# Earlier convolution steps, one product in fixed order, and room between statistics and norm rows in a gated long-convolution and SwiGLU layer

## The chip, the cores and the metric

The kernel runs on one core of a Trainium2 chip. Its time is device time in microseconds (us), the median of several runs. The engines named below are PE (TensorE, matrix products; PEld is its weight load), DVE (VectorE, elementwise), ACT (ScalarE, activations and casts), POOL (GpSimd) and SP (the engine whose queue issues the transfers). SBUF is the working memory of 128 partitions, PSUM the memory that PE writes its products to.

## The reference

A block of a transformer with 2048 tokens of 576 features, in two halves. The first is a long convolution along the tokens, the second a gated feed-forward layer with 4608 hidden features. Six rows (sa, ca, ga, sb, cb, gb) come from a condition vector.

```python
k_shift = sum_t k_pad[:, t:t+S, :] * shift_k[:, ks-1-t]        # 4 taps
kv = k_shift * v
y  = irfft(rfft(pad(kv)) * rfft(pad(ssm_k)))[:S] + kv * ssm_D  # causal, along the tokens
A(q, ...) = q * y
B(x) = (silu(x @ w1) * (x @ w3)) @ w2

h = layernorm(x) * (1 + ca) + sa
x = x + ga * A(h, k, v, shift_k, ssm_k, ssm_D)
h = layernorm(x) * (1 + cb) + sb
x = x + gb * B(h)
```

The layer norm has no weights of its own: it subtracts the mean and divides by sqrt(variance + 1e-5).

## The kernel before

The tokens are cut into eight blocks of 256 for the convolution and into four row blocks of 512 for the feed-forward layer. The convolution of a block works in a transformed domain: PE transforms the block's kv (spectrum X) and the block's filter (W, combined to V) by matrix products; block s is then the sum over j of X[j] * V[s - j], which DVE forms by one multiply and one add of 128 x 3456 elements for each pair; PE transforms the sum z back. So later blocks have more pairs. X and V of early blocks are written to memory and fetched again.

```python
def pair(self, X, V, s, last=False):
    nc = self.nc
    if s not in self.accs:                       # the first product of a block goes straight to z
        self.accs[s] = self.acc.tile([P, 6, D], BF16, name=f"z{s % 2}", tag=f"z{s % 2}")
        nc.vector.tensor_mul(self.accs[s][:], X[:], V[:])
        yield 2.0
        return
    z = self.accs[s]
    p = self.prod.tile([P, 6, D], BF16, name="p", tag="p")
    with self.behind(nc.vector) if last else nullcontext():
        nc.vector.tensor_mul(p[:], X[:], V[:])
    yield 2.0
    nc.vector.tensor_add(z[:], z[:], p[:])
    yield 2.0

def behind(self, engine):                        # what is traced inside comes after the engine's
    last = [i for i in self.nc.cur_bb.bb.instructions if i.engine == engine.engine][-1]
    return self.tc.issue_after(last)             # last traced instruction
```

The order of instructions on each engine is set when the kernel is built. A scheduler orders them by dependencies and by the order in which they are traced, and may move an instruction up; `behind` forbids that for what is traced inside it.

The convolution of the next two blocks is laid beside the feed-forward layer of the present row block. It is a generator: each `yield` says what its step costs in us; a negative number asks for so many us of other steps before it goes on, and `mix` takes these from a second generator. `advance` is called by the feed-forward code after each chunk of work and traces as many steps as its budget pays for.

```python
def advance(self, cost):
    self.due += cost
    while self.due > 0 and self.steps is not None:
        c = next(self.steps, None)
        if c is None:
            self.steps = None
            break
        self.due -= c
        self.spent += c
# in row_blocks: CONV_US = (72.0, 97.0, 108.0) for the convolution beside row blocks 0, 1, 2
            cost = CONV_US[r]
            time = 110.0 * 0.85 - (N1 * 1.03 if r == 0 else 0)
            rate = cost / time
# in stream(): the end of a chunk (128 hidden features for 512 tokens)
        def hide(k):
            ...
            nc.scalar.activation(h3, gus[k][:, 0, :].rearrange("p (a t) -> p a t", a=m), ACT.Silu)
            u = self.hp.tile([P, RB], BF16, name="u", tag="u")
            nc.scalar.copy(u[:], gus[k][:, 1, :])
            nc.vector.tensor_mul(h3, h3, u[:].rearrange("p (a t) -> p a t", a=m))
            del gus[k]
            self.advance(rate * 2.05)
# in down(): after each group of 16 products with w2; all steps that are left come at the sixth group of the second half
                if h == 1 and f0 // W2C == 5 and r + 1 < NRB:
                    self.end()
                    self.turn_all(2 * r + 3)
                ...
                self.advance(rate * W2C * 4 * 0.126)
```

A row block is `stream` (36 chunks: products with w1 and w3, L934 and L945, then silu, cast and product to h) and then `down` (products of h with w2, L1046, in two halves of 288 output features; L1063 reads a finished half from PSUM). The fourth row block runs in `stream_halves` (L1001), with no convolution beside it. PSUM holds four tiles of two banks. Each chunk takes one such tile, and so does each transform.

The last steps of a block of the convolution, `outcome`: the sums' real parts, back transform on PE, residual, statistics of the second norm on ACT, and the norm rows, which PE turns (L574) and which become the next row block's input.

```python
            yield self.real_parts(s)
            yield -waits[0]
            ...                                          # inverse transform, cast to y
            yield -waits[1]
            self.residual(s, y)
            yield 1.5
            if between is not None:
                between()
            ...                                          # (block 1 takes a quicker way here)
                sums = [...]
                for i in range(2):
                    with self.behind(nc.scalar):
                        self.ln_sums(self.xo[s], i, *sums)
                    yield 0.0
                yield -waits[2] / 2
                stats = self.ln_var(*sums, "l2")         # two DVE steps, then a power on POOL
                yield -waits[2] / 2
                r, b = self.ln_shift(*stats)             # one DVE step, l2n
                with self.behind(nc.scalar):
                    self.normed_act(s, r, b)             # four ACT instructions, h2row
            yield -waits[3]
```

The rows of the first norm are made the same way: `gate_stats`, `gate_var` (DVE, then POOL), and `gate_rows` (DVE's `ln_shift`, then two ACT instructions that write hg).

Of the kernel before, what the change touches and what calls it, by code (L numbers as in the profile page):

```python
# [32 lines left out]
N1 = 24  # L33
SPLIT = 2
EPS = 1e-5
EARLY_GETS = 6
# [8 lines left out]
class _Kernel:  # L45
# [277 lines left out]

    def kv_rows(self, s):

        nc = self.nc
        kh, vt = self.kh, self.vt
        kv = self.kvp.tile([P, 2, D], BF16, name="kv", tag="kv")
        tmp = self.kvp.tile([P, 2, D], BF16, name="kvt", tag="kvt")

        def tap(j):
            a = self.shk[:, j, :]
            return bass.AP(tensor=a.tensor, offset=a.offset, ap=[list(a.ap[0]), [0, 2], [1, D]])
        nc.vector.tensor_mul(kv[:], kh[:, 3:5, :], tap(0))
        yield 0.75
        for j in (1, 2, 3):
            nc.vector.tensor_mul(tmp[:], kh[:, 3 - j:5 - j, :], tap(j))  # L337
            nc.vector.tensor_add(kv[:], kv[:], tmp[:])  # L338
            yield 1.5
        nc.vector.tensor_mul(kv[:], kv[:], vt[:])  # L340
        self.kv = kv
        yield 0.75
# [40 lines left out]

    def v_block(self, s):

        nc = self.nc
        W = self.Wl[s]
        V = self.spec.tile([P, 6, D], BF16, name="V", tag="V")
        if s == 0:
            nc.vector.tensor_copy(V[:, 0:6:3, :], W[:, 0:4:2, :])  # L390
            VS = W[:, 1:4:2, :]
        else:
            Wp = self.Wl[s - 1]
            nc.vector.tensor_add(V[:, 0:6:3, :], W[:, 0:4:2, :], Wp[:, 1:4:2, :])
            nc.vector.tensor_sub(V[:, 1:6:3, :], W[:, 1:4:2, :], Wp[:, 0:4:2, :])
            VS = V[:, 1:6:3, :]
        nc.vector.tensor_add(V[:, 2:6:3, :], V[:, 0:6:3, :], VS)
        yield 2.25
        nc.vector.tensor_sub(V[:, 1:6:3, :], VS, V[:, 0:6:3, :])
        self.V[s] = V  # L400
        yield 0.75

    def pair(self, X, V, s, last=False):

        nc = self.nc
        if s not in self.accs:
            self.accs[s] = self.acc.tile([P, 6, D], BF16, name=f"z{s % 2}", tag=f"z{s % 2}")
            nc.vector.tensor_mul(self.accs[s][:], X[:], V[:])  # L408
            yield 2.0
            return  # L410
        z = self.accs[s]
        p = self.prod.tile([P, 6, D], BF16, name="p", tag="p")
        with self.behind(nc.vector) if last else nullcontext():
            nc.vector.tensor_mul(p[:], X[:], V[:])  # L414
        yield 2.0
        nc.vector.tensor_add(z[:], z[:], p[:])  # L416
        yield 2.0
# [58 lines left out]
    def center(self, dst, src, mean, rstd):  # L476
        self.nc.vector.tensor_scalar(dst, src, mean, rstd, op0=ALU.subtract, op1=ALU.mult)

    def behind(self, engine):

        last = [i for i in self.nc.cur_bb.bb.instructions if i.engine == engine.engine][-1]
        return self.tc.issue_after(last)
# [10 lines left out]
    def gate_var(self, s):  # L493
        self.l1[s] = self.ln_var(*self.l1[s])

    def gate_rows(self, s):

        x1 = self.xo[s]
        r, b = self.ln_shift(*self.l1.pop(s))
        hg = self.lnp.tile([P, 2, D], BF16, name="hg", tag="hg")  # L500
# [63 lines left out]

    def normed_act(self, s, r, b):
        row, x1 = self.h2row, self.xo[s]
        for cc in range(2):
            for lo, hi, at in ((0, D, 0), (512, D, D)):
# [170 lines left out]
    def outcome(self, s, fill, waits, between=None, quick=False):  # L739


        def steps():
# [19 lines left out]
            else:  # L762
# [7 lines left out]
                yield -waits[2] / 2  # L770
                r, b = self.ln_shift(*stats)
                with self.behind(nc.scalar):
                    self.normed_act(s, r, b)
            yield -waits[3]
# [11 lines left out]
    def conv_second(self):  # L786
        yield from self.gate_stats(1)
        yield from self.kv_rows(1)
        block = self.v_block(1)
        with self.behind(self.nc.vector):  # L790
            cost = next(block)
        yield cost

        def beside():
            yield from block
            self.gate_var(1)
            yield from self.pair(self.X[0], self.V[1], 1)
        yield from self.mix(self.x_spectrum(1), beside())
        self.mod_piece(5)
# [9 lines left out]
    def conv(self, s0):  # L809
        s1 = s0 + 1  # L810
# [12 lines left out]
        def old():  # L823
            V, X = self.old_v(s0 - 1, s0), self.old_x(1, s0)
            yield from self.pair(X, V, s0)
            for j in range(2, s0):
# [13 lines left out]
        def beside():  # L840
            yield from self.v_block(s1)
            with self.behind(self.nc.sync):
                self.load_kv(s1)
            yield from self.gate_stats(s1)
            if s0 > 2:
                yield from self.pair(X0, self.V[s0], s0)
            self.X1 = self.old_x(1, s0)
            yield from self.pair(X0, self.V[s1], s1)
            self.gate_var(s1)
            self.gate_rows(s0)  # L850
            yield from self.gate(s0)
# [8 lines left out]
        def others():  # L860
            yield from self.kv_rows(s1)
            yield from self.mix(self.x_spectrum(s1), more())
            yield from self.x_sums(s1)
# [35 lines left out]
    def stream(self, r, jobs, rate, size, finish=False):  # L899
# [49 lines left out]
        def hide(k):  # L949
# [7 lines left out]
            del gus[k]  # L957
            self.advance(rate * 2.05)

# [222 lines left out]
```

## Time and profile before

| what | value |
|---|---|
| time, median of 3 runs | 519.06 us (518.48 to 519.46) |
| profiled execution, span | 516.6 us |
| block 0 and set-up | about 0 to 34 us |
| row block 0, first half of its tokens, beside block 1 | about 34 to 67 us |
| row block 0, the rest of its products, beside blocks 2 and 3 | about 67 to 130 us, `down` to 170 |
| row block 1 beside blocks 4 and 5 | about 170 to 291 us, `down` from 248 |
| row block 2 beside blocks 6 and 7 | about 291 to 407 us, `down` from 369 |
| row block 3 | about 407 to 516 us, `down` from 477 |
| one large product or sum on DVE (128 x 3456) | 1.95 us |
| one DVE instruction of 128 x 1152 | 0.75 us |
| one chunk's silu and cast on ACT | 0.60 and 0.59 us |

How to read it: a line number such as L934 is a line of the kernel. In a timeline a line has the start in us, the length, the engine, the operation and what it writes and reads; in brackets stands how long the engine was idle just before it, and what ended that. A group's shape is partitions x elements. An engine's idle time costs something only where the chain that sets the end runs through it.

### The profile page before, as it was taken

To read this page: it belongs to the slowest core of one execution; us is meant where nothing else is said; L and a number is where in the kernel's file an instruction comes from. 1 tells how busy PE (TensorE), PEld (TensorE's weight loads), DVE (VectorE), ACT (ScalarE), POOL (GpSimd) and SP (SyncE) were. 2 spreads that over 40 slices of the span, in tenths; PEclk is the share of its full clock that TensorE was granted. 3 is DMA by queue.
4 is the path that set the end of the run, shared out by engine and by line. 5 is a ranking of instruction groups with operands and counts; after the bars stand their busy time and mean duration, and the time that the engine had idled before them with its cause. 6 is when DMAs were issued, how large, how long until landed. Compare 5 with 4: busy or idle time off the path is not lost.

```text
span 516.6 us, 9251 instructions
## 1 busy us (share of the span) xinstructions
PE 495.2 (96%) x3650; PEld 293.5 (57%) x3650; DVE 344.5 (67%) x557; ACT 293.6 (57%) x581; POOL 31.3 (6%) x75
## 2 busy tenths in 40 slices
PE   7899899989899999999998999999999999999997
PEld 3567665456688444344676643444578644444775
DVE  8888899999997354979999626988972222222012
ACT  7658589657543468769443464886815355555000
POOL 3100000002000000000101000020000000000000
PEclk9999999999999999999999999999999999999999
DMA  8957949686979866558997559854555545532462
GB/s 271 301 173 217 313 157 299 194 256 212 293 236 355 264 211 196 177 164 275 333 318 203 161 151 349 315 201 124 174 139 140 159 123 164 173 111 76 117 182 69
DMA packets 102207, 107.80 MB, mean 209 GB/s; under 512 B 5075, under 2 KB 94228, under 8 KB 102164
## 3 DMA queue, kind: packets, MB, share of 16 engines
q1 hardware_dynamic: 102142, 107.21, 67.3%
q8 instruction: 28, 0.46, 0.4%
q14 instruction: 15, 0.12, 0.1%
q10 hardware_dynamic: 22, 0.01, 0.0%
HBM read 96.00 MB, written 11.21 MB: 208 GB/s over the span
## 4 chain that ended last, share of the span: by engine, by line
PE 66%; DVE 21%; ACT 5%; DMA 3%; issue 3%; POOL 2%; SPq 0%; DVEq 0%; POOLq 0%; ACTq 0%
PE ps L934 24%; PE ps L1046 21%; PE ps L1001 12%; DVE p L414 4%; PE ps L945 4%; DVE z L416 3%; DVE z L408 2%; DVE h L956 2%; DMA kh<-in_A_k_dram 2%; PE ps L316 2%; POOL l2r L454 1%; DVE kv L338 1%; DVE kvt L337 1%; ACT junk L446 1%; DMA wst<-in_B_w_dram 1%
## 5 line engine op out<-in xcount | busy, mean ns | idle before, releaser
L934 PE MATMUL ps<-h2T,wst 128*128 128x512 bf16 (+1 forms) x1056 | 200.6, 341 | 1.1 <-ACT W L318 0.8
L934 PEld LDWEIGHTS <-wst 128*128 128x128 bf16 x1056 | 100.2, 98 | 85.7 <-issue 13.8
L1046 PE MATMUL ps<-wst,h 128*128 128x288 bf16 x1152 | 145.0, 286 | 3.9 <-ACT u L955 2.0
L1046 PEld LDWEIGHTS <-h 128*128 128x128 bf16 x1152 | 112.2, 98 | 33.3 <-issue 4.8
L953 ACT ACTIVATE h<-ps 128x512 bf16<-128x512 f32 x108 | 64.8, 600 | 67.6 <-PE ps L945 42.1
L1001 PE MATMUL ps<-h2T,wst 64*128 64x512 bf16 x648 | 70.3, 377 | 0.2 <-DMA wst<-in_B_w_dram 0.2
L956 DVE TENSOR_TENSOR h<-h,u 128x512 bf16<-128x512 bf16 x108 | 45.0, 421 | 36.3 <-ACT u L955 36.2
L955 ACT CAST u<-ps 128x512 bf16<-128x512 f32 x108 | 63.4, 587 | 0.0
L414 DVE TENSOR_TENSOR p<-X,V 128x3456 bf16<-128x3456 bf16 x28 | 54.7, 1954 | 4.2 <-DMA V<-Vd 2.2
L416 DVE TENSOR_TENSOR z<-z,p 128x3456 bf16<-128x3456 bf16 x28 | 54.7, 1954 | 0.2
L1001 PEld LDWEIGHTS <-wst 64*128 64x128 bf16 x648 | 31.5, 94 | 38.7 <-DMA wst<-in_B_w_dram 0.7
L1016 DVE TENSOR_TENSOR h<-h,u 128x512 bf16<-128x512 bf16 x36 | 15.3, 426 | 55.3 <-ACT u L1015 55.3
L1013 ACT ACTIVATE h<-ps 128x512 bf16<-128x512 f32 x36 | 21.5, 598 | 36.5 <-PE ps L1001 36.5
L1063 DVE TENSOR_TENSOR og<-ps,gbrow 128x288 bf16<-128x288 f32 x32 | 13.2, 451 | 41.1 <-PE ps L1046 41.1
L446 ACT ACTIVATE junk<-x 128x576 bf16<-128x576 bf16 x54 | 37.2, 689 | 0.5
L945 PE MATMUL ps<-h2T,wst 64*128 64x512 bf16 (+1 forms) x264 | 33.0, 342 | 0.0
L604 ACT ACTIVATE h2T<-ps,sbcol,cbcol 128x256 bf16<-128x256 bf16 x35 | 16.7, 569 | 19.4 <-PE ps L574 19.4
L569 ACT ACTIVATE h2row<-x,l2n,l2r 128x576 bf16<-128x576 bf16 (+1 forms) x24 | 13.7, 643 | 19.4 <-DVE l2n L460 19.4
L454 POOL TENSOR_TENSOR l2r<-l2v,neghalf 128x2 f32<-128x2 f32 x6 | 11.2, 1868 | 181.2 <-DVE l2v L453 181.2
L337 DVE TENSOR_TENSOR kvt<-kh,shk 128x1152 bf16<-128x1152 bf16 x24 | 18.1, 754 | 4.3 <-DMA kh<-in_A_k_dram 4.2
L1015 ACT CAST u<-ps 128x512 bf16<-128x512 f32 x36 | 20.9, 581 | 0.0
L945 PEld LDWEIGHTS <-wst 64*128 64x128 bf16 x264 | 8.5, 94 | 21.0 <-issue 20.8
(140 smaller groups left out, 398.6 us busy)
## 6 DMA issues: line engine op xcount, KB each, us to landing
wst<-in_B_w_dram SPq DMA_DIRECT2D x80, 512.0 KB, 5.0
wst<-in_B_w_dram SPq DMA_DIRECT2D x72, 288.0 KB, 3.4
X<-Xd SPq DMA_DIRECT2D x8, 864.0 KB, 6.7
Xd<-X SPq DMA_DIRECT2D x6, 864.0 KB, 6.0
wst<-in_B_w_dram SPq DMA_DIRECT2D x80, 64.0 KB, 3.3
kh<-in_A_k_dram SPq DMA_DIRECT2D x7, 720.0 KB, 7.3
Vd<-V SPq DMA_DIRECT2D x4, 864.0 KB
V<-Vd SPq DMA_DIRECT2D x4, 864.0 KB, 9.6
```

Of the source, the lines that this page charges most:

```text
L337: nc.vector.tensor_mul(tmp[:], kh[:, 3 - j:5 - j, :], tap(j))
L414: nc.vector.tensor_mul(p[:], X[:], V[:])
L416: nc.vector.tensor_add(z[:], z[:], p[:])
L446: self.nc.scalar.activation(junk[:], src[:, i, :], func, scale=scale, accum_out=out[:, col:col + 1])
L934: nc.tensor.matmul(gus[k][:, i, a * n:(a + 1) * n], w[:, 5 * i + ct, (fi + a) * P:(fi + a + 1) * P], hT[:, ct, t0:t1], start=(first and ct ...
L945: nc.tensor.matmul(gus[k][:, i, a * n:(a + 1) * n], w[rows, 4, (fi + a) * P:(fi + a + 1) * P], hT[rows, 4, t0:t1], start=(first and a == 0 ...
L953: nc.scalar.activation(h3, gus[k][:, 0, :].rearrange("p (a t) -> p a t", a=m), ACT.Silu)
L955: nc.scalar.copy(u[:], gus[k][:, 1, :])
L956: nc.vector.tensor_mul(h3, h3, u[:].rearrange("p (a t) -> p a t", a=m))
L1001: nc.tensor.matmul(gus[f][:, i, :], w[rows, 5 * i + ct if ct < 4 else 4, cols], hT[rows, ct, :], start=swap == 0 and ct == 0, stop=swap == ...
L1013: nc.scalar.activation(h3, gus[f][:, 0, :], ACT.Silu)
L1046: nc.tensor.matmul(acc[t], self.h3[:, f0 + f, t * P:(t + 1) * P], w[:, f, :], start=(f0 + f == 0), stop=(f0 + f == NF - 1))
```

## The change

It adds no work and takes none away; it changes when steps are traced and so in which order the engines do them. It has four parts.

- **Pace.** In row blocks 1 and 2 each of the first eight chunks pays for 1.8 times as many convolution steps as before; the later ones are unchanged. It is meant to use DVE's free time at the head of these stages.
- **Fixed order.** Block 2's first product is put behind DVE's last traced instruction, so that the scheduler can't move it in front of block 1's last sums. The helper `placed` is added for this; it is also used in `v_block` for block 1, where two instructions are held in place of three.
- **Statistics and norm rows of the second norm.** After `ln_shift`, 3 us of other steps are asked for, and 1 us after each half of the rows, so that ACT has other work while the statistics are finished.
- **Shift of the first norm.** `ln_shift` becomes a step of its own (`gate_shift`), some steps ahead of the rows that use it; the rows of block s0 move one product up.

```diff
@@ -32,6 +32,8 @@
 FIRST_DUE = 12.0
 N1 = 24
 SPLIT = 2
+HEAD = 8
+HEAD_PACE = 1.8
 EPS = 1e-5
 EARLY_GETS = 6
 
@@ -321,7 +323,7 @@
         nc.vector.tensor_add(both, both, odd)
         yield 1.5
 
-    def kv_rows(self, s):
+    def kv_rows(self, s, last=False):
 
         nc = self.nc
         kh, vt = self.kh, self.vt
@@ -331,10 +333,12 @@
         def tap(j):
             a = self.shk[:, j, :]
             return bass.AP(tensor=a.tensor, offset=a.offset, ap=[list(a.ap[0]), [0, 2], [1, D]])
-        nc.vector.tensor_mul(kv[:], kh[:, 3:5, :], tap(0))
+        with self.placed(last):
+            nc.vector.tensor_mul(kv[:], kh[:, 3:5, :], tap(0))
         yield 0.75
         for j in (1, 2, 3):
-            nc.vector.tensor_mul(tmp[:], kh[:, 3 - j:5 - j, :], tap(j))
+            with self.placed(last):
+                nc.vector.tensor_mul(tmp[:], kh[:, 3 - j:5 - j, :], tap(j))
             nc.vector.tensor_add(kv[:], kv[:], tmp[:])
             yield 1.5
         nc.vector.tensor_mul(kv[:], kv[:], vt[:])
@@ -381,7 +385,7 @@
             odd = self.kvp.tile([P, 2, D], BF16, name="Wo", tag="Wo")
             yield from self.forward2(self.Fk, self.kT, W[:, 0:2, :], odd[:], W[:, 2:4, :])
 
-    def v_block(self, s):
+    def v_block(self, s, last=False):
 
         nc = self.nc
         W = self.Wl[s]
@@ -391,8 +395,9 @@
             VS = W[:, 1:4:2, :]
         else:
             Wp = self.Wl[s - 1]
-            nc.vector.tensor_add(V[:, 0:6:3, :], W[:, 0:4:2, :], Wp[:, 1:4:2, :])
-            nc.vector.tensor_sub(V[:, 1:6:3, :], W[:, 1:4:2, :], Wp[:, 0:4:2, :])
+            with self.placed(last):
+                nc.vector.tensor_add(V[:, 0:6:3, :], W[:, 0:4:2, :], Wp[:, 1:4:2, :])
+                nc.vector.tensor_sub(V[:, 1:6:3, :], W[:, 1:4:2, :], Wp[:, 0:4:2, :])
             VS = V[:, 1:6:3, :]
         nc.vector.tensor_add(V[:, 2:6:3, :], V[:, 0:6:3, :], VS)
         yield 2.25
@@ -405,12 +410,13 @@
         nc = self.nc
         if s not in self.accs:
             self.accs[s] = self.acc.tile([P, 6, D], BF16, name=f"z{s % 2}", tag=f"z{s % 2}")
-            nc.vector.tensor_mul(self.accs[s][:], X[:], V[:])
+            with self.placed(last):
+                nc.vector.tensor_mul(self.accs[s][:], X[:], V[:])
             yield 2.0
             return
         z = self.accs[s]
         p = self.prod.tile([P, 6, D], BF16, name="p", tag="p")
-        with self.behind(nc.vector) if last else nullcontext():
+        with self.placed(last):
             nc.vector.tensor_mul(p[:], X[:], V[:])
         yield 2.0
         nc.vector.tensor_add(z[:], z[:], p[:])
@@ -476,6 +482,9 @@
     def center(self, dst, src, mean, rstd):
         self.nc.vector.tensor_scalar(dst, src, mean, rstd, op0=ALU.subtract, op1=ALU.mult)
 
+    def placed(self, last):
+        return self.behind(self.nc.vector) if last else nullcontext()
+
     def behind(self, engine):
 
         last = [i for i in self.nc.cur_bb.bb.instructions if i.engine == engine.engine][-1]
@@ -493,10 +502,13 @@
     def gate_var(self, s):
         self.l1[s] = self.ln_var(*self.l1[s])
 
+    def gate_shift(self, s):
+        self.l1[s] = self.ln_shift(*self.l1[s])
+
     def gate_rows(self, s):
 
         x1 = self.xo[s]
-        r, b = self.ln_shift(*self.l1.pop(s))
+        r, b = self.l1.pop(s)
         hg = self.lnp.tile([P, 2, D], BF16, name="hg", tag="hg")
         with self.behind(self.nc.scalar):
             for i in range(2):
@@ -562,9 +574,9 @@
         self.center(row[:, cc, 0:D], x1[:, cc, :], m, r)
         self.center(row[:, cc, D:640], x1[:, cc, 512:D], m, r)
 
-    def normed_act(self, s, r, b):
+    def normed_act(self, s, cc, r, b):
         row, x1 = self.h2row, self.xo[s]
-        for cc in range(2):
+        with self.behind(self.nc.scalar):
             for lo, hi, at in ((0, D, 0), (512, D, D)):
                 self.nc.scalar.activation(row[:, cc, at:at + hi - lo], x1[:, cc, lo:hi], ACT.Identity,
                                           bias=b[:, cc:cc + 1], scale=r[:, cc:cc + 1])
@@ -768,9 +780,11 @@
                 yield -waits[2] / 2
                 stats = self.ln_var(*sums, "l2")
                 yield -waits[2] / 2
-                r, b = self.ln_shift(*stats)
-                with self.behind(nc.scalar):
-                    self.normed_act(s, r, b)
+                scales = self.ln_shift(*stats)
+                yield -3.0
+                for cc in range(2):
+                    self.normed_act(s, cc, *scales)
+                    yield -1.0
             yield -waits[3]
             self.accs.pop(s)
             self.hg.pop(s)
@@ -786,15 +800,14 @@
     def conv_second(self):
         yield from self.gate_stats(1)
         yield from self.kv_rows(1)
-        block = self.v_block(1)
-        with self.behind(self.nc.vector):
-            cost = next(block)
-        yield cost
+        block = self.v_block(1, True)
+        yield next(block)
 
         def beside():
             yield from block
             self.gate_var(1)
             yield from self.pair(self.X[0], self.V[1], 1)
+            self.gate_shift(1)
         yield from self.mix(self.x_spectrum(1), beside())
         self.mod_piece(5)
         self.gate_rows(1)
@@ -822,7 +835,7 @@
 
         def old():
             V, X = self.old_v(s0 - 1, s0), self.old_x(1, s0)
-            yield from self.pair(X, V, s0)
+            yield from self.pair(X, V, s0, s0 == 2)
             for j in range(2, s0):
                 X = self.old_x(j, s0)
                 yield from self.pair(X, V, s1)
@@ -839,15 +852,16 @@
 
         def beside():
             yield from self.v_block(s1)
+            self.gate_shift(s0)
             with self.behind(self.nc.sync):
                 self.load_kv(s1)
             yield from self.gate_stats(s1)
             if s0 > 2:
                 yield from self.pair(X0, self.V[s0], s0)
             self.X1 = self.old_x(1, s0)
+            self.gate_rows(s0)
             yield from self.pair(X0, self.V[s1], s1)
             self.gate_var(s1)
-            self.gate_rows(s0)
             yield from self.gate(s0)
         yield from self.mix(self.x_spectrum(s0), beside())
         yield from self.x_sums(s0)
@@ -859,6 +873,7 @@
 
         def others():
             yield from self.kv_rows(s1)
+            self.gate_shift(s1)
             yield from self.mix(self.x_spectrum(s1), more())
             yield from self.x_sums(s1)
         yield from self.outcome(s0, others(), (5.0, 4.5, 6.0, 0.0), lambda: self.gate_rows(s1))
@@ -955,7 +970,7 @@
             nc.scalar.copy(u[:], gus[k][:, 1, :])
             nc.vector.tensor_mul(h3, h3, u[:].rearrange("p (a t) -> p a t", a=m))
             del gus[k]
-            self.advance(rate * 2.05)
+            self.advance(rate * 2.05 * (HEAD_PACE if r > 0 and k < HEAD else 1.0))
 
         def begin(k):
             if items[k][1] == 0:
```

## The prediction

> **What bounds the kernel now.** I read the page's first two parts, then the busy times by stretch of time, then TensorE's (PE's) own waits, then the timelines of VectorE (DVE), ScalarE (ACT) and PE around each wait.
>
> The page's first part, and two rows of its 40 slices:
>
> ```profile
> PE 495.2 (96%) x3650; PEld 293.5 (57%) x3650; DVE 344.5 (67%) x557; ACT 293.6 (57%) x581; POOL 31.3 (6%) x75
> PE   7899899989899999999998999999999999999997
> DVE  8888899999997354979999626988972222222012
> ```
>
> PE is busy for 96% of 516.6 us, so PE sets the time wherever it doesn't wait; DVE averages 67% but swings between 9 and 2 tenths. The busy times by stretch (start:end, length, then busy us of PE, PE weight loads, DVE, ACT, GpSimd) show where PE does wait:
>
> ```profile
> 55.00:60.00 5.00, 2.97 (x24) 2.26 (x24) 3.37 (x5) 2.69 (x6) 0.00 (x0) 1.00 0.93 267
> 60.00:100.00 40.00, 38.34 (x304) 24.90 (x302) 37.07 (x67) 32.79 (x68) 2.60 (x4) 1.00 0.72 230
> 100.00:138.00 38.00, 33.28 (x257) 21.59 (x255) 37.35 (x51) 24.13 (x47) 3.81 (x1) 1.00 0.83 252
> ...
> 170.00:187.00 17.00, 16.91 (x95) 7.32 (x94) 5.91 (x16) 10.57 (x19) 0.00 (x0) 1.00 0.81 249
> ...
> 247.00:291.00 44.00, 40.77 (x342) 31.88 (x340) 42.78 (x52) 18.91 (x37) 2.77 (x2) 1.00 0.84 262
> 291.00:320.00 29.00, 29.00 (x155) 11.95 (x153) 11.66 (x21) 17.05 (x31) 0.00 (x0) 1.00 0.69 223
> 320.00:400.00 80.00, 79.52 (x504) 44.73 (x503) 62.10 (x93) 51.69 (x108) 5.03 (x4) 1.00 0.61 189
> ```
>
> PE's idle time between 55 and 400 us, which is all that the change can touch, is 2.03 + 1.66 + 4.72 + 3.23 + 0.48 + 0.1 = **12.2 us**. It lies where DVE is nearly full (37.35 of 38; 42.78 of 44), not where DVE is at a third (5.91 of 17 at the head of row block 1, 11.66 of 29 at the head of row block 2). PE's own waits in that time, the large ones (us in total, times, longest):
>
> ```profile
> PE ps L542 <- DVE z L528: 2.6, 1, 2.6
> PE ps L1046 <- ACT u L955: 2.0, 2, 1.5
> PE ps L542 <- DVE z L524: 1.9, 1, 1.9
> PE ps L1046 <- DVE og L1063: 1.9, 1, 1.9
> ...
> PE ps L367 <- ACT u L955: 0.9, 1, 0.9
> ```
>
> Three kinds: the inverse transform (L542) waits for DVE's sums z; a matmul waits for ACT's cast u, which is the last reader of a PSUM tile; the second half of the down product (L1046) waits for DVE's og, which reads the first half's PSUM. The timelines show what stood in front. At 55 us:
>
> ```profile
> 55.07 1.95 DVE L408 TENSOR_TENSOR z<-X,V 128x3456 bf16<-128x3456 bf16 x1
> 56.94 0.75 DVE L524 TENSOR_TENSOR z<-z 128x1152 bf16<-128x1152 bf16 x1
> 57.75 1.63 PE L542 MATMUL ps<-z,Fb 128*128 128x288 bf16 x12 [1.87 <-DVE z L524]
> ```
>
> The L408 is block 2's first product, moved up by the scheduler between two steps of block 1's sums. At 123 us:
>
> ```profile
> 123.41 3.81 POOL L454 TENSOR_TENSOR l2r<-l2v,neghalf 128x2 f32<-128x2 f32 x1 [31.93 <-DVE l2v L453]
> 127.46 2.29 ACT L569 ACTIVATE h2row<-x,l2n,l2r 128x576 bf16<-128x576 bf16 x4 [3.47 <-DVE l2n L460]
> 130.75 1.02 PE L1046 MATMUL ps<-wst,h 128*128 128x288 bf16 x7 [1.55 <-ACT u L955]
> ```
>
> ACT sits 3.47 us before the norm rows (L569), waiting for GpSimd's power and DVE's l2n; behind it stand the casts that free PSUM; PE then waits 1.55.
>
> **What the Trainium skill says.** "Perfetto Trace Analysis", Identifying the Most-Contended Engine: the share of time that matmuls are busy is a poor measure of TensorE's distance to its limit, occupancy is fair for DVE and ACT. So I use PE's idle gaps with their releasers, and DVE's busy time. Same page, Optimization Strategy: where the limiting engine changes over time, interleaving the regimes can help; the pace of 1.8 does that, and the 5.91 of 17 beside 42.78 of 44 shows two such regimes. "SBUF — State Buffer", Who interferes with whom: a DVE instruction with two SBUF inputs contends with a GpSimd instruction that reads SBUF. The trace agrees: the same power takes 0.70 us at 90.78, with DVE idle, and 3.81 at 123.41 among DVE tensor-tensor instructions. So this wait is real and won't shrink by itself.
>
> **The change part by part.** No instruction is added or removed; only order moves, so PE's 495 us of work stays and the sum is over idle time.
>
> (1) Block 2's first product behind DVE's last traced instruction (`pair(X, V, s0, s0 == 2)`). It leaves 55.07, where it took 1.87 us up to L524's start, and lands among block 2's kv rows near 67 to 77. PE's wait of 1.87 at 57.75 goes. But from 60 to 138 DVE has only 2.93 + 0.65 = 3.6 us idle, and the product's 1.95 must be paid there: block 2's own inverse (wait 2.58 + 0.35 at 105) is released by DVE as late as before, less what DVE can absorb of its idle time; between 77 and 98 it has 1.8 us idle and I let it absorb half. PE comes there 1.9 earlier and waits some 0.9 longer. Net: **-1.0**. `v_block(1, True)` pins two instructions as before and leaves the third to follow them by data: 0. `kv_rows(last)` is never called with True: 0.
>
> (2) Steps between statistics and norm rows (`yield -3.0`, then two halves with -1.0 after each). ACT gets about 3 us of other work before L569. The casts that were held come 2 to 3 us earlier, so the 1.55 at 130.75 and the 0.93 at 251.02 (same picture: ACT idle 2.15 before L569 at 247.73) should go but for 0.2 or so each: **-1.3 and -0.7**. The price is up to 5 us more of step time in front of the transposes of the norm rows. For block 3 the rows end at 161.0 and PE turns them at 163.09; for block 5 they end at 283.2 and PE is there at 284.19, so the room is 2 and 1 us. The early shift takes block 5's forward; block 3 has none: **+0.3** as an estimate.
>
> (3) l1's shift as a step of its own, and the rows of hg one product earlier. DVE's waits for l1's power are short (0.81 at 42.33, 82.05 and 91.51) and lie beside PE's work: **-0.2**.
>
> (4) Pace 1.8 in the first eight chunks of row blocks 1 and 2. The step budget of a chunk is 2.05 x 97/93.5 = 2.13 us in row block 1 and 2.05 x 108/93.5 = 2.37 in row block 2; 0.8 of it, eight times, is **13.6 and 15.2 us** of steps moved forward. In row block 1 DVE idles 11.1 us from 170 to 187 and 8 us from 187 to 207, so it has the room. The full stretch from 247 to 291 loses that load: the wait for og (1.87 at 273.39) goes whole, the one for z at 259.03 (0.43) too: **-2.2**. In row block 2 only 0.48 is there to win, at 370.61, where ACT is crowded by the rows and statistics of block 7: **-0.3**. Against it: at the head, 30.6 us of steps are now traced within about 16.6 us of chunks, and what they need (X and V from memory) lands 6.7 and 9.6 us after its issue; in row block 2 DVE already waits 2.16 us for V at 319. PE's inverse is pulled up in its queue with the rest and can meet sums that are not done: **+0.8** as an estimate over both.
>
> Sum: -1.0 - 1.3 - 0.7 + 0.3 - 0.2 - 2.2 - 0.3 + 0.8 = -4.6 us. The whole is reordered by a scheduler, and such reorderings more often bring new small waits than take away unseen ones; I add 0.5. 519.06 - 4.1 = **515.0 us**.
>
> **The rivals.** (A) DVE is the bound of the stretch from 60 to 138, and the time before it cannot be used: PE arrives earlier and waits longer for z L528. For it: 97 to 98% DVE there. Against: products of blocks 4 and 5 (L408 at 109 and 142) are already done in that time, so the full DVE is in part filled with work that isn't due. It would take away (1) whole: 516. (B) The early steps collide with loads or with ACT: PE meets an inverse or spectrum whose input is late, and a wait of 2 to 5 us appears in row block 1 or 2. For it: buffers for three X and four V only, and loads of 864 KB beside weights at up to 349 GB/s in one of the page's slices. Against: block 6's kv row is finished at 284, long before its spectrum at 331, and DVE has room. It would make 517 to 521. (C) All waits go, also the 2.58 at 105, because gate work moves off that chain: 519.06 - 11 = 508, the best there is.
>
> **Range and chances.** The 12.2 us of idle time is a ceiling; faster by over 2% needs 10.4 of it, so rival C nearly whole: 0.05. Slower by over 2% needs 10.4 us of new waits, against one to five in rival B: 0.02. Between lies 0.93. The range is 510.8 (all that (1) to (4) could win at best, 1.87 + 2.48 + 0.2 + 2.78 = 7.3, and 1 of the z wait) to 519.4 (rival B eats the whole gain).
>
> **What would show each step right or wrong.** (1): no L408 between L522 and L524 of block 1, PE's wait for z L524 under 0.4; the wait for z L528 in its place longer, about 3.5. (2): ACT's wait at h2row, 19.4 us in all five, under 10; PE's waits at L1046 and L367 for ACT u under 0.6 together. (4): DVE above 10 of 17 us busy in the first 17 us of row block 1, no PE wait for og, and no new PE wait above 1 us at L316 or L542 in row blocks 1 and 2. I am wrong if PE's idle time between 55 and 400 us doesn't fall by 3 us or more; new waits at L542 in row block 1 or 2 would be rival B.

## The result, and the profile after

The changed kernel takes **519.85 us** (median, 519.49 to 520.91) beside 518.79 (518.48 to 519.46) for the kernel before on the same chip: ratio **1.0022**, interval 1.0003 to 1.0041. The prediction was 515.0. The change gives no gain; it costs about 1 us. Line numbers move with the diff: L542 is now L554, L1046 is L1061, L1063 is L1078, L528 is L540, L569 is L581; in the other kernels below the same operations have slightly different numbers.

The page of the kernel after, its first part and two rows of its slices (DVE is the second row; the last is the granted clock of PE in tenths):

```profile
PE 498.4 (96%) x3650; PEld 294.8 (57%) x3650; DVE 345.5 (67%) x557; ACT 292.9 (57%) x581; POOL 26.1 (5%) x75
...
DVE  8888799999997287989999637998711222221012
...
PEclk9999999989999999999999999999999999999999
```

The same work is done, as promised, but PE is busy 3.2 us longer. One slice of the clock row has an 8. Busy time by stretch of the kernel after (columns as before: PE, PE weight loads, DVE, ACT, GpSimd, then the granted clock):

```profile
55.00:60.00 5.00, 4.72 (x41) 3.59 (x38) 3.21 (x7) 3.44 (x6) 0.00 (x0) 1.00 0.85 253
60.00:100.00 40.00, 38.10 (x300) 24.08 (x298) 37.97 (x67) 32.34 (x67) 2.72 (x4) 1.00 0.76 241
100.00:138.00 38.00, 34.03 (x256) 22.51 (x257) 37.07 (x48) 23.14 (x45) 0.69 (x1) 0.96 0.70 220
138.00:170.00 32.00, 30.05 (x253) 23.64 (x252) 26.88 (x34) 13.63 (x28) 1.13 (x1) 1.00 0.92 296
170.00:187.00 17.00, 17.00 (x100) 7.99 (x97) 8.19 (x19) 10.08 (x18) 0.00 (x0) 1.00 0.80 241
...
207.00:247.00 40.00, 37.76 (x199) 15.43 (x198) 36.51 (x50) 27.92 (x56) 0.69 (x1) 1.00 0.79 264
247.00:291.00 44.00, 43.59 (x347) 32.35 (x345) 42.21 (x46) 18.16 (x36) 2.33 (x1) 1.00 0.79 241
```

Length minus PE's busy time is its idle time. 55 to 60 fell from 2.03 to 0.28 and 247 to 291 from 3.23 to 0.41, as meant. But 138 to 170, which had none, now has 1.95 (1.41 for og, the rest for weights), and 207 to 247 has 2.24. From 55 to 400 the idle time is 11.3 us after 12.2: it fell by 0.9 where 3 or more was the mark. And from 100 to 138 the clock is 0.96, where it was 1.00: part of the longer busy time is slow work. PE's waits show what the new idle time is:

```profile
PE ps L554 <- DVE z L540: 3.7, 1, 3.7
...
PE ps L1061 <- DVE og L1078: 1.4, 1, 1.4
PE ps L318 <- DVE kv L344: 1.3, 1, 1.3
PE ps L1061 <- DMA wst<-in_B_w_dram: 0.9, 3, 0.4
PE ps L949 <- DMA wst<-in_B_w_dram: 0.9, 1, 0.9
```

No wait for ACT's u in the down product is left, and the 1.87 for block 1's z is gone. The wait for og is back, but in another place: in the kernel before it was at 273 us, here it stands at 154.7, in row block 0. The wait for block 2's z is 3.7, the 3.5 that step (1) named plus 0.2. The spectrum (L318) waits for kv in row block 1, and weights come late in four places. Where the time is lost shows in the first products of row block 0's `down` and of row block 1, first in the kernel before and then after:

```profile
130.75 4.08 PE L1046 MATMUL ps<-wst,h 128*128 128x288 bf16 x32 [1.55 <-ACT u L955]
169.52 0.81 PE L934 MATMUL ps<-h2T,wst 128*128 128x512 bf16 x3
```

```profile
129.90 6.04 PE L1061 MATMUL ps<-wst,h 128*128 128x288 bf16 x48
171.45 0.81 PE L949 MATMUL ps<-h2T,wst 128*128 128x512 bf16 x3
```

That stage takes 41.6 us in place of 38.8.

### The profile page after: what moved, and what is told of

Same layout as the page of the kernel before. It is cut to its first block, busy times and chain, and to the rows that moved or that the text cites. A ratio compares the mean times of both kernels' runs of the same rounds, so it can differ in the third digit from the quotient of the medians.

```text
span 517.8 us, 9255 instructions
## 1 busy us (share of the span) xinstructions
PE 498.4 (96%) x3650; PEld 294.8 (57%) x3650; DVE 345.5 (67%) x557; ACT 292.9 (57%) x581; POOL 26.1 (5%) x75
## 4 chain that ended last, share of the span: by engine, by line
PE 70%; DVE 20%; DMA 4%; ACT 3%; issue 2%; POOL 1%; SPq 0%; DVEq 0%; POOLq 0%; ACTq 0%
PE ps L949 24%; PE ps L1061 22%; PE ps L1016 14%; PE ps L960 4%; DVE p L420 3%; DMA wst<-in_B_w_dram 3%; DVE z L422 3%; DVE h L971 2%; PE ps L318 2%; DVE z L414 1%; DVE kv L342 1%; DVE kvt L341 1%; PE ps L253 1%; DMA knat<-in_A_ssm_k_dram 1%; ACT junk L452 1%
## 5 line engine op out<-in xcount | busy, mean ns | idle before, releaser
L1061 PE MATMUL ps<-wst,h 128*128 128x288 bf16 x1152 | 145.1, 286 | 2.4 <-DVE og L1078 1.4
L1061 PEld LDWEIGHTS <-h 128*128 128x128 bf16 x1152 | 112.3, 98 | 32.0 <-issue 3.1
L1078 DVE TENSOR_TENSOR og<-ps,gbrow 128x288 bf16<-128x288 f32 x32 | 13.1, 449 | 50.5 <-PE ps L1061 50.5
L581 ACT ACTIVATE h2row<-x,l2n,l2r 128x576 bf16<-128x576 bf16 (+1 forms) x24 | 14.0, 660 | 13.4 <-DVE l2n L466 13.4
L342 DVE TENSOR_TENSOR kv<-kv,kvt 128x1152 bf16<-128x1152 bf16 x24 | 18.1, 754 | 0.4
```

The costliest lines, as they stand in the source:

```text
L1061: nc.tensor.matmul(acc[t], self.h3[:, f0 + f, t * P:(t + 1) * P], w[:, f, :], start=(f0 + f == 0), stop=(f0 + f == NF - 1))
```

## The experiments

### The four parts, each alone

Each kernel is the one before with one part of the diff. Shortened:

```diff
 only_fix:    + yield from self.pair(X, V, s0, s0 == 2)    and placed() with its uses
 only_pace:   + self.advance(rate * 2.05 * (HEAD_PACE if r > 0 and k < HEAD else 1.0))
 only_room:   + yield -3.0 after ln_shift; each half of the norm rows, then yield -1.0
 only_shift:  + gate_shift() as a step; gate_rows(s0) one product earlier
```

> The kernel before with block 2's first product in fixed order, nothing else. Theory (parts act apart, each gives back what it wins at the next wait): PE's wait of 1.87 us at the inverse of block 1 goes, and PE then waits about 1.1 us longer, near 3.7 us, at the inverse of block 2, after which the granted clock falls to half for some 3 us as in the changed kernel (1.3 us lost): time +0.3 to +0.8 us against before. Rival (the long wait at block 2 comes from the earlier shift and rows, not from this part): wait there near 2.6 us, no drop of the clock, time -1.0 to -1.9.

**Measured:** 0.9983 (0.9975 to 0.9992), that is -0.9 us. PE's waits in this kernel no longer have the 1.87 for block 1's z, and the one for block 2's z is 3.5 in place of 2.6. Both waits and the size are those of step (1). But a third wait has gone that the prediction booked under step (2): the 1.55 for ACT's u ahead of row block 0's down product, though ACT's order is that of the kernel before. PE comes there later, after slow matmuls (see the last section). The down product still begins 0.05 us after that cast of u ends, and this is 0.8 us earlier than before, counted from row block 0's first product, because ACT's norm rows, which wait for DVE, are that much earlier. So it is DVE and ACT that set the gain here, and that it agrees with a sum of PE's waits may in part be luck.

> The kernel before with pace 1.8 in the first eight chunks of row blocks 1 and 2 alone. Theory: the waits for og (1.87) and z (0.43) in row block 1's down product go, and new waits of 2.5 to 3 us come in its chunks (kv near 219, a weight transfer near 244): time -0.8 to +0.3. Rival (the pace is sound, the new waits come from the longer step list of the room part): -1.5 to -2.5. Second rival (the pace is what made the changed kernel slower): +1 to +2.

**Measured:** 0.9959 (0.9945 to 0.9972), -2.1 us. The waits for og and for z in row block 1 are gone. The 0.93 for ACT's u at 251, booked under step (2), has gone with them. New are small waits for weights: 1.0 us at 243.9, and 1.5 in three in row block 0's down product, where the pace doesn't act yet.

> The kernel before with the steps between second-norm statistics and norm rows alone. Theory: the waits for ACT u at the start of the down product of row block 0 (1.55 us) and at the filter transposes (0.93) go, and about 2 us come back at the start of the second half of that down product, because block 2's norm rows are turned some 4 us later and hold a PSUM tile there: time -1.0 to +0.3. Rival (those 2 us come from the other parts): no wait for og or weights near 150 us in row block 0, time -1.8 to -2.6.

**Measured:** 1.0059 (1.0041 to 1.0077), +3.1 us, where step (2) had -1.7. The waits for ACT that step (2) named are gone, and the down product of row block 0 starts 2.3 us earlier, counted from that row block's first product. Then PE stands still for 4.4 us, and in row block 1 for another 1.4. PE's timeline of only_room (its L1057 and L1074 are the down product and og, L583 turns the norm rows):

```profile
149.26 0.72 PE L583 MATMUL ps<-ident,h2row 128*128 128x128 bf16 x10
149.82 1.63 PE L1057 MATMUL ps<-wst,h 128*128 128x288 bf16 x12
155.84 10.41 PE L1057 MATMUL ps<-wst,h 128*128 128x288 bf16 x70 [4.38 <-DVE og L1074]
```

and the same place in the kernel before:

```profile
146.85 0.72 PE L574 MATMUL ps<-ident,h2row 128*128 128x128 bf16 x10
147.41 4.82 PE L1046 MATMUL ps<-wst,h 128*128 128x288 bf16 x38
```

Before, PE turns block 2's norm rows 32 products ahead of the second half of the down product; the turn's PSUM tile is free again by then. In only_room the turn comes directly ahead of that half. A half takes two of the four tiles. The turn occupies one, and the second half has to take one that DVE's og still has to read: 12 of its products run first, then PE waits. DVE's timeline of only_room shows that og is late, behind products and sums:

```profile
149.22 1.95 DVE L422 TENSOR_TENSOR z<-z,p 128x3456 bf16<-128x3456 bf16 x1
...
152.43 1.95 DVE L420 TENSOR_TENSOR p<-X,V 128x3456 bf16<-128x3456 bf16 x1
154.30 0.75 DVE L323 TENSOR_TENSOR W<-W,Wo 128x1152 bf16<-128x1152 bf16 x1
154.97 0.82 DVE L1074 TENSOR_TENSOR og<-ps,gbrow 128x288 bf16<-128x288 f32 x2
```

PE had finished the first half when the turn began, at about 149.3; og begins at 154.97.

> The kernel before with the first norm's shift as its own step and the rows one product earlier, alone. Theory: PE's order is that of before, DVE's waits for l1's power move, nothing on PE's path: -0.3 to +0.3. Rival (the rows of hg taken earlier crowd DVE ahead of block 2's sums): wait at block 2's inverse up from 2.6 to over 3.3 us and time +0.7 to +2.

**Measured:** 1.0036 (1.0021 to 1.005), +1.9 us, where step (3) had -0.2. The order on PE is that of the kernel before; only DVE and ACT are reordered. Row block 1 waits 2.6 us for og (1.87 before), with slow matmuls behind it (see the last section).

The four changes in per cent add to -0.17 - 0.41 + 0.59 + 0.36 = +0.37; together they measure +0.22, which is the same within the noise. That the parts act apart isn't shown by it: og's wait in row block 0 is 4.4 us in only_room and 1.4 in the whole change.

### The two that gain, together, and the wait that is left

> Fixed order and pace, without the room before the norm rows and without the shift step. Theory (the two halves of the change act in opposite ways, near to additive): -0.17% and -0.41% add up, -2.5 to -3.5 us against before. Rival (fixed order only moves the wait and pace's gain was the same gain): -1.5 to -2.2 us, no better than pace alone.

**Measured:** 0.9948 (0.9933 to 0.9963), 516.6 us after 519.67: about the sum of the two. No kernel of the study is faster; that it is faster than the pace alone isn't certain, as the intervals overlap. PE's idle time from 55 to 400 us is 8.9 us in it, 3.3 below the kernel before. PE's waits of fix_pace:

```profile
PE ps L551 <- DVE z L537: 3.5, 1, 3.5
...
PE ps L1053 <- DMA wst<-in_B_w_dram: 1.3, 3, 0.7
```

No wait for og and none for ACT's u in the down products is left. The 3.5 at block 2's inverse is the largest. Two kernels try to get it, first by tracing the inverse later:

```diff
             yield -waits[0]
+            if s == 2:
+                yield 3.0
 ...
-  outcome(s0, others(), (5.0, 4.5, 6.0, 0.0), ...)
+  outcome(s0, others(), (5.0, 1.5 if s0 == 2 else 4.5, 6.0, 0.0), ...)
```

> As fix_pace, and block 2's inverse transform is traced 3 us of steps later (3 us less after it). Theory (PE's wait of 2.6 to 3.7 us there is a matter of place in PE's order, and the half clock after it follows from the wait): wait under 1 us, granted clock full at 100 to 112 us, a further -2 to -4 us against fix_pace. Rival (DVE bounds the stretch from 60 to 138 us, so PE only waits elsewhere): the wait turns up again before 138 us, time within 0.8 us of fix_pace.

**Measured:** 1.0004 (0.9989 to 1.0019). The wait for z is gone, and these, 6.9 us together, stand in its place:

```profile
PE ps L318 <- ACT X L320: 5.1, 1, 5.1
PE ps L318 <- DVE kv L344: 1.8, 1, 1.8
```

The second is meant to take work off DVE ahead of that inverse, by tracing block 3's first product behind it:

```diff
-            yield from self.pair(X0, self.V[s1], s1)
+            if s0 > 2:
+                yield from self.pair(X0, self.V[s1], s1)
 ...
         def more():
+            if s0 == 2:
+                yield from self.pair(X0, self.V[s1], s1)
```

> Fixed order and pace, and block 3's first product (1.95 us on DVE at 88 us, ahead of block 2's sums) is traced after block 2's inverse. Theory (PE's wait of 3.5 us at block 2's inverse is DVE work that isn't due yet): wait 1.5 to 2 us shorter, the half clock after it rarer, -1.5 to -3.5 us against fix_pace. Rival (DVE full from 60 to 138, so the product is paid before block 3's inverse): wait moves there, within 0.8 us of fix_pace.

**Measured:** 1.0003 (0.999 to 1.0015), 2.7 us worse than fix_pace. The wait for z is 3.0 in place of 3.5, and a wait of 1.8 for kv comes behind it. But the edit didn't move the product. DVE's timelines of fix_pace and of fix_pace_z3 have it at the same place:

```profile
87.02 1.96 DVE L414 TENSOR_TENSOR z<-X,V 128x3456 bf16<-128x3456 bf16 x1
```

```profile
87.05 1.96 DVE L414 TENSOR_TENSOR z<-X,V 128x3456 bf16<-128x3456 bf16 x1
```

It can only be block 3's, since block 4's first product writes the z tile that block 2's inverse still reads at 104. The scheduler took it up again, and only smaller steps changed places. So this kernel doesn't test the theory; against it speaks fix_pace_late2 alone. In fix_pace DVE is busy 75.36 of the 78 us from 60 to 138. That what one wait of PE loses there another gains, rival A of the prediction, fits this but isn't shown by these two.

### The new wait for og: when the steps are traced, or the tile

One theory was that too many steps are traced within the first half of the down product, ahead of og. This edit holds back those of its last three groups:

```diff
-                self.advance(rate * W2C * 4 * 0.126)
+                cost = rate * W2C * 4 * 0.126
+                if h == 0 and f0 // W2C > 5:
+                    self.due += cost
+                else:
+                    self.advance(cost)
```

> The room alone, with the same three groups held. Theory: the wait of 4.4 us for og in row block 0 falls below 1 us and the one in row block 1 (1.6) too, the half clock after it goes as well: -4 to -6 us against the room alone, so -1 to -3 against before. Rival (the tile of the turned rows): within 1 us of the room alone, +2 to +4 against before.

**Measured:** 1.004 (1.0025 to 1.0056); only_room was 1.0059. The largest wait of PE in this kernel:

```profile
PE ps L318 <- DVE og L1078: 3.2, 1, 3.2
```

It still waits for og, now at a filter's transform, which takes the tile in the half's stead.

> The changed kernel, with the convolution steps of the last three groups of the first half of each down product held back and traced in the second half. Theory (room costs because steps traced late in that half stand ahead of og on DVE, and the second half's PSUM tile waits for og): the waits for og (1.4 us in row block 0) go, -1 to -3 us against the changed kernel, so -2 to 0 against before. Rival (the PSUM tile of the turned norm rows is what is missing, not DVE's order): the wait at the start of the second half stays and moves to ACT h2T; no gain.

**Measured:** 1.0006 (0.9995 to 1.0018), with 1.0 us of wait for og at a filter's transform and 0.8 at the turn of block 2's rows. Holding steps moves the wait to another user of PSUM. The rival, the tile, has block 2's rows turned earlier:

```diff
-        yield from self.outcome(s1, ahead, (5.0, 4.5, 5.0, 0.0), lambda: self.turn_all(s0))
+        self.turn_all(s0)
+        yield from self.outcome(s1, ahead, (5.0, 4.5, 5.0, 0.0))
```

> The room alone, and the norm rows of the first block of each pair are turned just ahead of the second block's last steps instead of within them. Theory (the room cost its time because the turn fell right in front of the second half of row block 0's down product and took the PSUM tile that the half needs, so that the half got a tile released by DVE's og): no wait for og in row block 0, the 1.55 at its start stays away, -4 to -6 us against the room alone, -1 to -3 against before. Rival (DVE's backlog in that stretch is what PE waits for, whichever tile it gets): a wait of 2 us or more stays between 150 and 170 us, time within 1.5 us of the room alone (+1.5 to +3 against before).

**Measured:** 0.9974 (0.9959 to 0.9988), 4.6 us below only_room (517.95 after 522.52) by these two lines. The turn is at 131.81. PE's timeline then has no wait where the second half in row block 0 begins, though DVE's og comes as late as in only_room:

```profile
146.85 15.84 PE L1058 MATMUL ps<-wst,h 128*128 128x288 bf16 x128
```

```profile
154.28 0.81 DVE L1075 TENSOR_TENSOR og<-ps,gbrow 128x288 bf16<-128x288 f32 x2
```

Up to og, DVE's order is that of only_room. In row block 1, 0.5 of the 1.4 us for og is left. So the tile that the turn takes, and not DVE's backlog, is the cause of the loss, and with it out of the way part (2) gains 1.4 us, near the 1.7 of the prediction.

> The changed kernel with the same early turn. Theory: its 1.4 us for og and the small weight waits around it in row block 0 go: -1.5 to -2.5 us against the changed kernel, -0.5 to -1.5 against before. Rival: no change against the changed kernel (+0.5 to +1.5 against before).

**Measured:** 0.9987 (0.9978 to 0.9995): the whole change with the early turn is 0.35% below the change as it is.

> Fixed order, pace and room with the early turn, without the shift step. Theory (parts add: fix and pace -2.9, room's own gain with the turn -1 to -2): -4 to -5 us against before, the best so far. Rival (what room wins is the same time that pace wins): -2.5 to -3.5.

**Measured:** 0.9948 (0.9931 to 0.9964), the same as fix_pace. Room and pace win the same time, it seems: once the pace is there, the room adds nothing that can be measured, and the 0.93 at 251 is one wait that each takes away alone.

> The best version so far (fixed order and pace, 0.9948 of the time before) with block 2's norm rows turned ahead of block 3's outcome rather than inside it. Theory: the early turn only helps where the steps between statistics and norm rows moved the turn against the second half of the down product; without them the second half waits for ACT already and not for og, so this is at 0.994 to 0.996. Rival: the early turn relieves the PSUM tiles in any case; then it is at 0.992 or below.

**Measured:** 1.0005 (0.9991 to 1.0019), 2.9 us or so worse than fix_pace. The early turn is no gain by itself. PE's waits of fix_pace_turn show two that fix_pace doesn't have:

```profile
PE ps L583 <- ACT h2row L578: 1.8, 3, 0.7
...
PE ps L1054 <- ACT h2T L613: 0.7, 1, 0.7
```

Without the room the rows aren't ready when PE turns them. Both together are 2.5 us; that they make up the whole difference is likely, not shown.

### Which half of the third part costs

```diff
 shift_step = only_shift with the rows at their old place
-            self.gate_rows(s0)
             yield from self.pair(X0, self.V[s1], s1)
             self.gate_var(s1)
+            self.gate_rows(s0)
 shift_rows = the kernel before with gate_rows(s0) one product earlier, ln_shift inside it
```

> The kernel before with half of the third part: the first norm's shift is a step of its own some steps ahead, the rows of block s0 stay where they were. Both halves alone made 1.0036 of the time before. Theory S: the early shift is the cause, because DVE's queue[...] then meets an instruction that waits for GpSimd's power while products stand behind it; then this kernel is at 1.003 to 1.005, with a wait of DVE for GpSimd at L481 in it that the kernel before doesn't have, and PE's wait of about 2.6 for og in row block 1. Theory R, the rival: the rows' place is the cause; then this kernel is within 0.1% of before.

**Measured:** 1.0029 (1.0015 to 1.0042).

> The kernel before with the other half of the third part: the rows of block s0 are traced one product earlier, with their shift inside them as before. Theory R: the rows' place is the cause of the 1.0036; then this kernel is at 1.003 to 1.005 and shows the waits for og (about 2.6) in row block 1 and for ACT's y (1.6) in row block 2. Theory S: it is within 0.1% of before. If both halves are near 1.002, the two add up, and it is the reordering as such rather than one instruction.

**Measured:** 1.0006 (0.9994 to 1.0018). The early shift is the cause, as theory S had it, but not in its way: DVE's wait for GpSimd's power at l1n is 5.2 us in seven places in shift_step and in the kernel before alike. What changed is the order of all that DVE does after it. DVE's timeline of shift_step ahead of og in row block 1:

```profile
254.02 0.42 DVE L971 TENSOR_TENSOR h<-h,u 128x512 bf16<-128x512 bf16 x1
...
273.19 0.75 DVE L341 TENSOR_TENSOR kvt<-kh,shk 128x1152 bf16<-128x1152 bf16 x1
273.85 0.75 DVE L402 TENSOR_TENSOR V<-V 128x1152 bf16<-128x1152 bf16 x1
274.52 0.81 DVE L1078 TENSOR_TENSOR og<-ps,gbrow 128x288 bf16<-128x288 f32 x2
```

and of the kernel before:

```profile
271.85 0.75 DVE L397 TENSOR_TENSOR V<-V 128x1152 bf16<-128x1152 bf16 x1
272.52 0.82 DVE L1063 TENSOR_TENSOR og<-ps,gbrow 128x288 bf16<-128x288 f32 x2
...
277.46 0.75 DVE L337 TENSOR_TENSOR kvt<-kh,shk 128x1152 bf16<-128x1152 bf16 x1
```

One h and one instruction of the kv rows (kvt) more stand ahead of og, which begins 2.0 us later: 0.9 by which DVE was behind already at 250, and 1.1 more, nearly all of it these two. PE itself was 1.25 later at that point, so its wait grows by 0.74, from 1.87 to 2.61. At the start of row block 1 PE is 3.0 us behind: 1.5 of it is a new wait for kv at 112.3 and 1.4 two waits for weights, of which it isn't shown that the shift brings them. Why moving one short step reorders these, rather than others, is the scheduler's doing and isn't settled.

## Why the prediction was wrong, step by step

- **The premise of the sum failed in part**: PE's busy time didn't stay at 495 us but is 498.4. Slow clock makes up 1.3 of it in the trace; the rest isn't traced.
- **Step (1), fixed order, was right in size and in its two waits**: -0.9 for -1.0. The wait moved from block 1's z to block 2's, 1.87 going and 0.9 coming back, as worked out. That this difference alone makes the gain isn't shown (only_fix).
- **Step (4), pace, was right** and somewhat better, -2.1 for a net -1.7. But DVE's first 17 us of row block 1 rose from 5.91 to 8.19 and not above 10 as I had put it; the next 20 us rose from 12.03 to 16.39. In the whole change a wait for kv of 1.3 us at 219.8 appears in row block 1, the kind that rival B named; alone, the pace doesn't have it.
- **Step (2) failed, in its last term, "+0.3 as an estimate"** for the price of the room. The two terms for the waits held: both went, though the 1.55 is gone in only_fix and only_pace and the 0.93 in only_pace too, so they weren't the room's alone to win. The price was taken from the time between the end of the rows and their turn by PE, so from whether the rows come in time. The turn isn't late for its own data. It is late for PSUM: 2.4 us later it stands directly ahead of the second half of the down product and takes a tile of it, and the half waits 4.4 us for og (only_room; 1.4 in the whole change). The term measured +3.1 + 1.7 = 4.8 us in place of 0.3, part of it slow clock (below). only_room_turn, which takes away this alone, brings the gain back. ACT's wait for the norm rows, which I had put at under 10, came down less too; the kernel after:

```profile
ACT h2row L581 <- DVE l2n L466: 13.4, 3, 7.2
```

- **Step (3) failed: "lie beside PE's work: -0.2"**. It measured +1.9. The short waits for GpSimd do lie beside PE's work, and moving the shift has no worth there. But a step that is moved changes the order of the DVE instructions behind it (shift_step 1.0029), and where DVE is nearly full og and kv then come later. Part of the +1.9 is slow clock behind og's wait. The 0.5 for reordering stood for this and was a quarter of it.
- **Rival A** held for the stretch from 60 to 138, not as far as taking away step (1) whole; the last section has a case where 1.6 us of slower matmuls there cost nothing. **Rival B** came in the sum, 519.85 in its 517 to 521, but mostly by another way: by a PSUM tile in row block 0 and by DVE's order behind the shift, more than by loads or spectra in row blocks 1 and 2.

## What to carry to other kernels

When a step is moved to give one engine room, follow every buffer that the moved step takes as well as the data it waits for: the next user of the same pool may then depend on a much slower reader. Where an engine is nearly full, take only the parts of a reordering whose releaser you can name in the trace, and time each alone: here two of four gave -0.5%, and the other two took it all away.

## What the runs showed of the hardware that was not expected

PE's granted clock halves after some of these waits, so that the matmuls behind a wait take longer. The kernel after, stretches of 2 us around block 2's inverse (the first number after the five engines is the clock):

```profile
104.00:106.00 2.00, 0.45 (x3) 0.29 (x4) 2.00 (x5) 0.00 (x0) 0.00 (x0) 0.80 1.08 374
106.00:108.00 2.00, 1.78 (x8) 0.88 (x7) 2.00 (x5) 0.64 (x1) 0.00 (x0) 0.50 0.07 22
108.00:110.00 2.00, 2.00 (x17) 1.53 (x14) 2.00 (x3) 0.64 (x1) 0.00 (x0) 0.85 0.00 0
```

and its PE timeline there:

```profile
105.56 1.12 PE L554 MATMUL ps<-z,Fb 128*128 128x288 bf16 x4 [3.72 <-DVE z L540]
```

At half clock for 0.8 + 2.0 + 0.6 = 3.4 us, four matmuls take 1.12 us; in the kernel before, without it, they take 0.65. The matmuls of this stretch take about 1.3 us longer in all, more than PE's idle time fell. only_room has the same 3.4 us after its 4.38 us wait: 70 matmuls take 10.41 us there, while at the pace of the 38 in 4.82 they would take 8.9. In only_shift it falls on og's wait in row block 1; below it the same matmuls in the kernel before:

```profile
273.61 12.61 PE L1061 MATMUL ps<-wst,h 128*128 128x288 bf16 x88 [2.62 <-DVE og L1078]
```

```profile
273.39 10.97 PE L1046 MATMUL ps<-wst,h 128*128 128x288 bf16 x88 [1.87 <-DVE og L1063]
```

Whether slow matmuls cost the kernel time depends on what PE meets next. Up to 170 us, only_pace has the order of the kernel before on PE, DVE and ACT. Its trace has 3.4 us of half clock from 106.6, which the trace of the kernel before hasn't. The lines of only_pace, then those of the kernel before (its down product begins at 130.75, shown above):

```profile
106.66 3.55 PE L943 MATMUL ps<-h2T,wst 128*128 128x256 bf16 x16
129.89 0.57 ACT L964 CAST u<-ps 128x512 bf16<-128x512 f32 x1
130.51 4.08 PE L1055 MATMUL ps<-wst,h 128*128 128x288 bf16 x32
```

```profile
106.87 1.91 PE L934 MATMUL ps<-h2T,wst 128*128 128x256 bf16 x16
130.13 0.57 ACT L955 CAST u<-ps 128x512 bf16<-128x512 f32 x1
```

Both begin the down product 0.05 us after this cast ends, 97.1 us after row block 0's first product (at 33.41 and 33.64). The 1.55 us that PE waits for ACT's u in the kernel before is gone instead: at this point DVE and ACT set the time, not PE. Half clock doesn't tell the good kernels from the bad ones either: fix_pace has twice as much of it as the kernel after (0.91 over 38 us, so 6.8 us at half).

```profile
100.00:138.00 38.00, 34.42 (x253) 22.64 (x253) 37.35 (x49) 23.71 (x46) 3.82 (x1) 0.91 0.76 229
```

The Trainium skill, "TensorE: Matmul & The Clock Gate", What's actually happening, says that the array falls to half clock after an idle window of some 3.4 us, and HAM oscillation — how this bites in real kernels gives as its rule that PE shouldn't idle for more than that. The traces agree on the half, and slow stretches last 3.4 or 6.8 us in them. But shorter waits are hit too: shift_rows' matmuls take 1.12 us after a wait of 2.46, while in the kernel before they take 0.65 after 2.58. In timed runs of only_shift with a mean clock of 1.0 the mean is 520.04 us (3 runs), with 0.993 it is 521.54 (5 runs); of the kernel before, timed beside shift_step, 519.54 at 0.999 or more (12 runs), 519.50 at 0.995 to 0.998 (21 runs) and 520.14 at 0.993 (2 runs). Whether a given wait is hit varies between runs, so the share of this in the +0.22% isn't settled.
